# Attention decode on one core: tiles of 8 MB with 64 KB rows in a ring of three, shared by K, V and the projection weights

## The chip, the cores and the metric

The kernel runs on one core of a Trainium2 chip. The metric is the device time of one execution in microseconds (us), lower is better; a median over several executions is quoted. The profile's span is about 2 us shorter than the measured time of the same execution (2602.3 against 2604.1 us for the kernel before).

In the text, PE is the matmul engine, VectorE (DVE in the profile) does elementwise work and reductions, ScalarE (ACT) does exp and copies, SP is the engine whose queue issues the loads. "The DMA" means the 16 DMA engines that move data from HBM, the main memory, into SBUF, the memory on the core (128 partitions, its rows).

## The reference

Two independent problems A and B of the same shape; the outputs are concatenated. Every query attends to 4096 cached keys.

```python
B, Sq, D = 8, 1, 1024
H, Sk, Dh = 32, 4096, 128          # all bf16

def _A_ref(x, k_cache, v_cache, wq, wo):
    q = (x @ wq).reshape(B, Sq, H, Dh).transpose(0, 2, 1, 3)
    scores = jnp.einsum("bhqd,bhkd->bhqk", q, k_cache) * (Dh ** -0.5)
    p = softmax(scores, axis=-1)
    o = jnp.einsum("bhqk,bhkd->bhqd", p, v_cache)
    return o.transpose(0, 2, 1, 3).reshape(B, Sq, H * Dh) @ wo
# B_ref is the same on its own inputs; result: concatenate([a, b], axis=-1)
```

The caches are 4 x 268 MB, and wq and wo are 4 x 8.4 MB. Each byte is used once, so the kernel has to read 1107 MB.

## The kernel before

A tile holds four heads of one batch entry: 128 partitions, 32 partitions a head, T = 128 keys of 128 values in each partition, so 32 KB a partition and 4 MB a tile. K and V tiles alternate through a ring of five slots. One transfer loads one tile, and it may start when the tile that held the slot before, five tiles ago, has been used up:

```python
HQ = 4; MP = 128 // HQ; T = Sk // MP; CT = 32; NR = T // CT    # four chunks a tile
NSLOT = 5
order = [("k", 0)]
for n in range(NQ - 3):
    order += [("k", n + 1), ("v", n)]
...
def freed(i):                       # what has to be done before a slot is loaded anew
    kind, n = order[i]
    return opEacc.get(NR * n + NR - 1) if kind == "k" else opPV.get((n, NR - 1))
...
from_ = caches[c][...][b, hb * HQ:(hb + 1) * HQ].rearrange("u (m t) d -> (u m) (t d)", m=MP)
op = dma(to, from_, ("t", i % NSLOT), [dep])                   # 128 rows of 32 KB
```

For each of the chunks of a K tile, VectorE multiplies by q in place, reduces the partial sums of the chunk before, and folds 128 products to 64; PE sums the 64 to 16 with four identity matmuls. K's slot is free when the last chunk's matmuls have read it:

```python
make_mul(s)            # VectorE: ring *= q           128x4096
make_red(s - 1)        # VectorE: 16 partial sums to 1, of the chunk before
fold = make_fold(s)    # VectorE: ring[:64] += ring[64:]
...
make_eacc(s, fold)     # PE: red += identity @ ring, four times; the last reader of the chunk
```

The softmax follows on ScalarE, then PE multiplies by V. The weights have buffers of their own and come in rows of 2 KB: wq in 8 pieces of 2 MB, wo in 16 pieces of 1 MB.

```python
opWQ[m] = dma(WQ[:], caches[c][3][:, col:col + HM * Dh].rearrange("(k p) n -> p k n", p=128), ...)
opWO[blk] = dma(WO[:], caches[c][4][hb * HQ * Dh:(hb + 1) * HQ * Dh, :].rearrange("(h p) n -> p h n", p=128), ...)
```

Of the kernel before, what the change touches and what calls it, by code (L numbers as in the profile page):

```python
# [81 lines left out]

def _build_kernel(nc, caches, out):
# [3 lines left out]
    assert B == 8 and Sq == 1 and Dh == 128 and Sk == 4096 and D == 1024 and H % 8 == 0  # L87
    DC = D // 128
    scale = float(Dh) ** -0.5
    HQ = 4  # L90
# [4 lines left out]
    HM = 2 * HQ  # L95
    MPC = H // HM
    NM = NC * MPC
    NB = NC * H // HQ
    NQ = NB * B
    NS = NQ * NR  # L100
    NSLOT = 5
    PL = 7
    RG = T // 4 // 4

    es = ExitStack()
    with es:
# [3 lines left out]

        ident = sb("ident", [128, 128], BF16)
        mask = sb("mask", [128, HQ], FP32)
        E16 = sb("E16", [128, 4, HQ], BF16)
        selb = sb("selb", [B, B, MP], BF16)
        x_sb = sb("x_sb", [B, NC, D], BF16)
        xT = sb("xT", [128, NC * DC * B], BF16)
        WQ = sb("WQ", [128, DC, HM * Dh], BF16)
        WO = sb("WO", [128, HQ, D], BF16)
        q_sb = sb("q_sb", [B, 4, HQ * Dh], BF16)
        qbc = sb("qbc", [128, 2, Dh], BF16)  # L120
        ring = sb("ring", [128, NSLOT, T * Dh], BF16)
        s_sb = sb("s_sb", [128, 3, T], FP32)
        rmax = sb("rmax", [128, 2], FP32)
        ngm = sb("ngm", [128, 2], FP32)
        bias = sb("bias", [128, 2], FP32)
        rsum = sb("rsum", [128, 2, B], FP32)
        PM = sb("PM", [128, 3, T, HQ], BF16)
        accS = sb("accS", [128, 2, 512], BF16)
        rl = sb("rl", [128, 2, HQ * B], FP32)
        on_sb = sb("on_sb", [128, 2, HQ, B], BF16)  # L130
        orow = sb("orow", [64, 512], BF16)

        red_ps = [ps(f"red{i}") for i in range(2)]
        pv_ps = [ps(f"pv{i}") for i in range(2)]
        o_ps = [ps(f"o{i}") for i in range(2)]
        misc = ps("misc")
        proj = ps("proj")
        misc_bf16 = misc.bitcast(BF16)

        sems = {e: es.enter_context(nc.semaphore(f"c_{e}")) for e in ENGINES[1:]}  # L140
        for name, n in (("t", NSLOT), ("vl", NR), ("wq", 1), ("wo", 1), ("x", 1), ("out", 1)):
            for i in range(n):
                sems[(name, i)] = es.enter_context(nc.semaphore(f"{name}{i}"))
# [4 lines left out]
        def dma(out_ap, in_ap, key, deps):  # L148
            return add("sp", lambda e: e.dma_start(out_ap, in_ap), deps, dma_key=key)


        def pool_select(view, base, pattern, dep):
            return add("pool", lambda e: e.affine_select(out=view, in_=view, compare_op=ALU.not_equal, fill=1.0,
                                                         base=base, pattern=pattern, channel_multiplier=1), [dep])
        z = [add("pool", lambda e, m=m: e.memset(m[:], 0.0)) for m in (ident, selb, E16, mask)]
        c_ident = pool_select(ident[:], 0, [[-1, 128]], z[0])
        c_selb = pool_select(selb[:], 0, [[-1, B], [0, MP]], z[1])

        c_E16 = z[2]
        for q in range(4):  # L160
            c_E16 = pool_select(E16[:], -32 * q, [[-4, 4], [-1, HQ]], c_E16)
        c_mask = z[3]
        for j in range(HQ):
            c_mask = add("dve", lambda e, j=j: e.memset(mask[MP * j:MP * (j + 1), j:j + 1], 1.0), [c_mask])
        c_PM = add("pool", lambda e: e.memset(PM[:], 0.0))
        c_pv = [add("dve", lambda e, t=t: e.memset(t[:], 0.0)) for t in pv_ps]

        opT, opMul, opEacc, opRed, opRmax, opNgm, opBias, opExp = {}, {}, {}, {}, {}, {}, {}, {}
        opPV, opAcc, opExt, opQb, opQbc, opQ, opQs, opWQ, opWO = {}, {}, {}, {}, {}, {}, {}, {}, {}
        opLsum, opNorm, opProj = {}, {}, {}  # L170
        last = {"misc": None}
        outs = []



        order = [("k", 0)]
        for n in range(NQ - 3):
            order += [("k", n + 1), ("v", n)]
        order += [("k", NQ - 2), ("k", NQ - 1), ("v", NQ - 3), ("v", NQ - 2), ("v", NQ - 1)]
# [6 lines left out]
        def freed(i):  # L186

            kind, n = order[i]
            return opEacc.get(NR * n + NR - 1) if kind == "k" else opPV.get((n, NR - 1))

        def load_tiles():
            while issued[0] < len(order):
                i = issued[0]
                dep = None
                if i >= NSLOT:
                    dep = freed(i - NSLOT)
                    if dep is None:
                        return
                kind, n = order[i]
                blk, b = divmod(n, B)  # L200
                c, hb = divmod(blk, H // HQ)
                from_ = caches[c][1 if kind == "k" else 2][b, hb * HQ:(hb + 1) * HQ].rearrange("u (m t) d -> (u m) (t d)", m=MP)
                to = tile_of(kind, n)
                if i == len(order) - 1:
                    for r in range(NR):
                        cols = slice(r * CT * Dh, (r + 1) * CT * Dh)
                        opT[("v", n, r)] = dma(to[:, cols], from_[:, cols], ("vl", r), [dep])
                else:
                    op = dma(to, from_, ("t", i % NSLOT), [dep])
                    for r in range(NR):  # L210
                        opT[(kind, n, r)] = op
                issued[0] += 1

        def load_wq(m):
            c, p = divmod(m, MPC)
            col = p * HM * Dh
            opWQ[m] = dma(WQ[:], caches[c][3][:, col:col + HM * Dh].rearrange("(k p) n -> p k n", p=128),
                          ("wq", 0), [_at(opQ, (m - 1, 1))])

        def load_wo(blk):  # L220
            c, hb = divmod(blk, H // HQ)
            opWO[blk] = dma(WO[:], caches[c][4][hb * HQ * Dh:(hb + 1) * HQ * Dh, :].rearrange("(h p) n -> p h n", p=128),
                            ("wo", 0), [_at(opProj, blk - 1)])


        def make_q(m, f):

            c = m // MPC
            blk = 2 * m + f

            def emit(e):
                for k in range(DC):
                    i = e.matmul(misc[0:B, :], xT[:, (c * DC + k) * B:(c * DC + k + 1) * B],  # L233
                                 WQ[:, k, f * HQ * Dh:(f + 1) * HQ * Dh], start=(k == 0), stop=(k == DC - 1))
                return i
            opQ[(m, f)] = add("pe", emit, [c_xT, opWQ[m], last["misc"]])
            opQs[blk] = last["misc"] = add(
                "act", lambda e: e.activation(q_sb[:, blk % 4, :], misc[0:B, :], ACTF.Copy),  # L238
                [opQ[(m, f)], _at(opQb, (blk - 4) * B + B - 1)])

        def make_qbc(n):

            blk, b = divmod(n, B)

            def emit(e):
                for j in range(HQ):
                    i = e.matmul(misc[MP * j:MP * (j + 1), 0:Dh], selb[:, b, :], q_sb[:, blk % 4, j * Dh:(j + 1) * Dh],  # L247
                                 start=True, stop=True, tile_position=(0, MP * j))
                return i
            opQb[n] = add("pe", emit, [c_selb, opQs[blk], last["misc"]])  # L250
# [18 lines left out]
        def make_eacc(s, fold):  # L269
            v = chunk(*divmod(s, NR)).rearrange("p (t j w) -> p t j w", j=8, w=16)  # L270
# [6 lines left out]
            opEacc[s] = add("pe", emit, [fold, c_ident, _at(opRed, s - 2)])  # L277

        def make_red(s):
            n, r = divmod(s, NR)  # L280
            opRed[s] = add("dve", lambda e: e.tensor_reduce(  # L281
                s_sb[:, n % 3, r * CT:(r + 1) * CT], red_ps[s % 2][:, :].rearrange("p (t w) -> p t w", w=16), AX.X, ALU.add),
                [opEacc[s]] + _at(opExp, n - 3, []))


        def make_rmax(n):
            opRmax[n] = add("dve", lambda e: e.tensor_reduce(rmax[:, n % 2:n % 2 + 1], s_sb[:, n % 3, :], AX.X, ALU.max),  # L287
                            [opRed[NR * n + NR - 1]])

        def make_ngm(n):  # L290
            opNgm[n] = add("dve", lambda e: e.tensor_reduce(  # L291
                ngm[:, n % 2:n % 2 + 1], rmax[:, n % 2:n % 2 + 1].to_broadcast([128, 32]), AX.X, ALU.max,
                negate=True, apply_transpose=True), [opRmax[n], _at(opBias, n - 2)])

        def make_exp(n):
            blk, b = divmod(n, B)
            opBias[n] = add("act", lambda e: e.activation(bias[:, n % 2:n % 2 + 1], ngm[:, n % 2:n % 2 + 1], ACTF.Copy, scale=scale),  # L297
                            [opNgm[n]] + _at(opExp, n - 2, []))
            opExp[n] = []
            for j in range(HQ):  # L300
                rows = slice(MP * j, MP * (j + 1))

                def emit(e, j=j, rows=rows):
                    return e.activation(PM[rows, n % 3, :, j], s_sb[rows, n % 3, :], ACTF.Exp, bias=bias[rows, n % 2:n % 2 + 1],  # L304
# [187 lines left out]
```

## Time and profile before

| | before |
|---|---|
| time, median | 2603.8 us (2603.3 to 2604.4) |
| HBM read | 1107 MB, 426 GB/s over the span |
| VectorE / PE / ScalarE busy | 80% / 53% / 17% |
| packets of the DMA | 54,248 |

From the page of the kernel before. The first two lines are the busy tenths of VectorE and of the DMA in 40 slices of the span, then what the DMA moved in each slice, its packets, and the chain of waits by engine. Of the groups (line, engine, operation, tiles, count, busy us, mean ns, idle us before it and what ended it) two are shown, and of the issues (queue, count, size, median us from issue to landing) the loads of K and V.

```profile
DVE  7778887788878878788787887878878788788887
DMA  9999999999999999999999999999999999999997
GB/s 410 427 429 430 431 427 429 431 429 432 425 430 431 430 429 428 431 429 432 429 424 431 430 430 431 427 430 432 429 431 421 428 433 427 433 429 431 430 430 314
DMA packets 54248, 1108.58 MB, mean 426 GB/s; under 512 B 4577, under 2 KB 4609, under 8 KB 21009
...
DMA 70%; DVE 22%; PE 7%; ACT 1%; issue 1%; SPq 0%
...
L262 DVE TENSOR_TENSOR ring<-ring,qbc 128x4096 bf16<-128x4096 bf16 x512 | 1165.9, 2277 | 476.0 <-DMA ring<-in_A_k_cache_dram 247.4
...
L304 ACT ACTIVATE PM<-s_sb,bias 32x128 bf16<-32x128 f32 x512 | 295.0, 576 | 15.1
...
ring<-in_A_k_cache_dram SPq DMA_DIRECT2D x64, 4096.0 KB, 39.9
ring<-in_A_v_cache_dram SPq DMA_DIRECT2D x64, 4096.0 KB, 31.4
```

The DMA is busy in every slice, and VectorE's idle time, 476 us, ends on landings of K: the DMA is the limit. A K tile takes 9.7 us to move, but it lands 39.9 us after its issue. So it is issued while about three other tiles still stand in the queue before it. The queue is never near dry.

The trace also holds each packet of the DMA with its bytes and duration. A row of a tile is one packet:

```
bytes of a packet   count    mean ns
 2,048              16,400      88
32,768              32,640    1219
```

### The profile page before, as it was taken

How to read it: one execution, taken by the hardware profiler on the slowest of the kernel's cores; microseconds unless marked ns; L12 is line 12 of the kernel's file. 1: busy time of each engine (PE TensorE's matmuls, PEld its weight loads, DVE VectorE, ACT ScalarE, POOL GpSimd, SP SyncE). 2: the span in 40 equal slices, each digit the busy share in tenths (PEclk: the TensorE clock that was granted, in tenths of full speed). 3: DMA queues.
4: the chain of work that ended last, by engine and by line, in shares of the span. 5: the costliest groups of instructions: out<-in, count | busy, mean ns of one | idle time of the engine just before them, and what ended most of it. 6: DMA issues, size and time to landing. Idle time of an engine off the chain costs nothing.

```text
span 2602.3 us, 18878 instructions
## 1 busy us (share of the span) xinstructions
PE 1383.7 (53%) x7568; PEld 384.3 (15%) x7568; DVE 2086.1 (80%) x1833; ACT 445.7 (17%) x1427; POOL 3.6 (0%) x15
## 2 busy tenths in 40 slices
PE   4455564554545555455554555545555455454555
PEld 1111111111111111111111111111111111111111
DVE  7778887788878878788787887878878788788887
ACT  1112111121111111121111211112111121121112
POOL 0000000000000000000000000000000000000000
PEclk8666666666666667666666666666666666666666
DMA  9999999999999999999999999999999999999997
GB/s 410 427 429 430 431 427 429 431 429 432 425 430 431 430 429 428 431 429 432 429 424 431 430 430 431 427 430 432 429 431 421 428 433 427 433 429 431 430 430 314
DMA packets 54248, 1108.58 MB, mean 426 GB/s; under 512 B 4577, under 2 KB 4609, under 8 KB 21009
## 3 DMA queue, kind: packets, MB, share of 16 engines
q1 hardware_dynamic: 54160, 1107.38, 99.5%
q8 instruction: 59, 0.97, 0.2%
q14 instruction: 29, 0.23, 0.0%
HBM read 1107.33 MB, written 0.03 MB: 426 GB/s over the span
## 4 chain that ended last, share of the span: by engine, by line
DMA 70%; DVE 22%; PE 7%; ACT 1%; issue 1%; SPq 0%
DMA ring<-in_B_k_cache_dram 31%; DMA ring<-in_A_k_cache_dram 30%; DVE ring L262 12%; DVE ring L267 6%; DMA ring<-in_A_v_cache_dram 4%; DMA ring<-in_B_v_cache_dram 4%; PE red L275 3%; DVE s_sb L281 3%; PE pv L317 2%; ACT PM L304 1%; PE proj L357 1%; PE o L338 0%; PE misc L233 0%; DVE rmax L287 0%; ACT accS L323 0%
## 5 line engine op out<-in xcount | busy, mean ns | idle before, releaser
L262 DVE TENSOR_TENSOR ring<-ring,qbc 128x4096 bf16<-128x4096 bf16 x512 | 1165.9, 2277 | 476.0 <-DMA ring<-in_A_k_cache_dram 247.4
L275 PE MATMUL red<-ring,ident 128*128 128x512 bf16 x2048 | 887.2, 583 | 992.2 <-DVE ring L267 992.2
L267 DVE TENSOR_TENSOR ring<-ring 128x2048 bf16<-128x2048 bf16 x512 | 622.0, 1215 | 0.0
L275 PEld LDWEIGHTS red<-ring,ident 128*128 128x128 bf16 x2048 | 214.3, 127 | 1461.9 <-DVE ring L267 1204.1
L317 PE MATMUL pv<-ring,PM 128*16 128x512 bf16 x4096 | 398.7, 505 | 7.1 <-DMA ring<-in_A_v_cache_dram 4.5
L281 DVE TENSOR_REDUCE s_sb<-red 128x32 f32<-128x512 f32 x512 | 350.0, 684 | 16.7 <-PE red L275 16.7
L297 ACT ACTIVATE bias<-ngm 128x1 f32<-128x1 f32 x128 | 26.0, 203 | 1590.2 <-DVE ngm L291 1590.2
L304 ACT ACTIVATE PM<-s_sb,bias 32x128 bf16<-32x128 f32 x512 | 295.0, 576 | 15.1
L331 PE MATMUL o<-E,accS 128*128 128x4 bf16 x512 | 34.1, 171 | 206.0 <-ACT accS L323 205.9
L317 PEld LDWEIGHTS pv<-ring,PM 128*16 128x16 bf16 x4096 | 99.6, 101 | 282.1 <-issue 236.8
L304 ACT ACTIVATION_READ_ACCUMULATOR PM<-s_sb,bias 32x1 f32 x512 | 128.1, 250 | 0.0
L252 ACT ACTIVATE qbc<-misc 128x128 bf16<-128x128 f32 x128 | 35.5, 278 | 385.9 <-PE misc L247 385.9
L323 ACT ACTIVATE accS<-pv 128x512 bf16<-128x512 f32 x128 | 76.4, 597 | 6.2 <-PE pv L317 2.8
L331 PEld LDWEIGHTS o<-E,accS 128*128 128x128 bf16 x512 | 23.5, 107 | 314.2 <-ACT accS L323 314.2
L287 DVE TENSOR_REDUCE rmax<-s_sb 128x1 f32<-128x128 f32 x128 | 36.6, 286 | 4.5
L247 PE MATMUL misc<-q_sb,selb 8*32 8x128 bf16 x512 | 37.3, 282 | 0.8 <-ACT q_sb L238 0.8
L233 PE MATMUL misc<-WQ,xT 128*8 128x512 bf16 x128 | 32.8, 402 | 6.2 <-DMA WQ<-in_A_wq_dram 6.2
L238 ACT ACTIVATE q_sb<-misc 8x512 bf16<-8x512 f32 x16 | 9.4, 587 | 143.1 <-PE misc L233 143.1
L247 PEld LDWEIGHTS misc<-q_sb,selb 8*32 8x32 bf16 x512 | 13.4, 96 | 106.5 <-issue 106.5
L338 PE MATMUL o<-rsum,mask 128*128 128x8 f32 x128 | 28.9, 354 | 0.0
L338 PEld LDWEIGHTS o<-rsum,mask 128*128 128x128 f32 x128 | 27.7, 319 | 0.0
L291 DVE TRANSPOSE_TENSOR_REDUCE ngm<-rmax 128x1 f32<-128x32 f32 x128 | 26.2, 204 | 0.0
(25 smaller groups left out, 59.2 us busy)
## 6 DMA issues: line engine op xcount, KB each, us to landing
ring<-in_A_k_cache_dram SPq DMA_DIRECT2D x64, 4096.0 KB, 39.9
ring<-in_A_v_cache_dram SPq DMA_DIRECT2D x64, 4096.0 KB, 31.4
ring<-in_B_k_cache_dram SPq DMA_DIRECT2D x64, 4096.0 KB, 40.4
ring<-in_B_v_cache_dram SPq DMA_DIRECT2D x63, 4096.0 KB, 31.8
WQ<-in_A_wq_dram SPq DMA_DIRECT2D x4, 2048.0 KB, 41.5
WO<-in_A_wo_dram SPq DMA_DIRECT2D x8, 1024.0 KB, 38.1
WQ<-in_B_wq_dram SPq DMA_DIRECT2D x4, 2048.0 KB, 44.3
WO<-in_B_wo_dram SPq DMA_DIRECT2D x8, 1024.0 KB, 37.6
```

The source lines that it names most:

```text
L247: i = e.matmul(misc[MP * j:MP * (j + 1), 0:Dh], selb[:, b, :], q_sb[:, blk % 4, j * Dh:(j + 1) * Dh], start=True, stop=True, tile_position ...
L252: "act", lambda e: e.activation(qbc[:, n % 2, :], misc[:, 0:Dh], ACTF.Copy),
L262: opMul[s] = add("dve", lambda e: e.tensor_tensor(v, v, qbc[:, n % 2, :].unsqueeze(1).to_broadcast([128, CT, Dh]), ALU.mult), [opT[("k", n ...
L267: return add("dve", lambda e: e.tensor_tensor(v[:, :, 0:64], v[:, :, 0:64], v[:, :, 64:128], ALU.add), [opMul[s]])
L275: i = e.matmul(dst, ident[:], v[:, :, j, :], start=(j == 0), stop=(j == 3))
L281: opRed[s] = add("dve", lambda e: e.tensor_reduce(s_sb[:, n % 3, r * CT:(r + 1) * CT], red_ps[s % 2][:, :].rearrange("p (t w) -> p t w", w ...
L287: opRmax[n] = add("dve", lambda e: e.tensor_reduce(rmax[:, n % 2:n % 2 + 1], s_sb[:, n % 3, :], AX.X, ALU.max), [opRed[NR * n + NR - 1]])
L304: return e.activation(PM[rows, n % 3, :, j], s_sb[rows, n % 3, :], ACTF.Exp, bias=bias[rows, n % 2:n % 2 + 1], scale=scale, accum_out=rsum ...
L317: i = e.matmul(bank[32 * q:32 * q + 4 * HQ, :], PM[:, n % 3, t:t + 4, :].rearrange("p t j -> p (t j)"), v[:, t * Dh:(t + 4) * Dh], start=( ...
L323: opAcc[n] = add("act", lambda e: e.activation(accS[:, n % 2, :], pv_ps[n % 2][:], ACTF.Copy), [opPV[(n, NR - 1)], _at(opExt, n - 2)])
L331: x = e.matmul(o_ps[blk % 2][:, HQ * b:HQ * (b + 1)], accS[:, n % 2, i * 128:(i + 1) * 128], E16[:, i, :], start=(i == 0), stop=(i == 3))
L338: x = e.matmul(o_ps[blk % 2][:, 64 + B * j:64 + B * (j + 1)], mask[:, j:j + 1].to_broadcast([128, 128]), rsum[:, blk % 2, :], start=True, ...
```

## The change

The intent is longer rows. A tile becomes eight heads of one batch entry, 16 partitions a head: 64 KB a partition and 8 MB a tile, in eight chunks of the same size as before. Only three such slots fit in SBUF, and wq and wo have no room of their own any more. They go through the ring too, each whole weight matrix as one tile with rows of 64 KB. The last eight heads of the last wo stay apart (2 MB in rows of 2 KB), so the second wo is loaded into 96 partitions only. Around this the softmax changes form: exp runs eight times over 128 partitions, with a scale of 0 and a bias of -200 for partitions of other heads, instead of four times over 32.

```diff
-    HQ = 4
+    HQ = 8
...
-    NSLOT = 5
-    PL = 7
+    NSLOT = 3
...
-        order = [("k", 0)]
-        for n in range(NQ - 3):
-            order += [("k", n + 1), ("v", n)]
-        order += [("k", NQ - 2), ("k", NQ - 1), ("v", NQ - 3), ("v", NQ - 2), ("v", NQ - 1)]
+        order = [("wq", 0), ("k", 0)]
+        late = {}
+        for n in range(NQ):
+            if n == 0:
+                order += [("wq", c) for c in range(1, NC)]
+            if n + 1 < NQ:
+                order.append(("k", n + 1))
+            for c in range(NC):
+                if n == done_at(c, NC, HB, B) + 1:
+                    order.append(("wo", c))
+                    late[n] = c
+            if n == NQ - 1:
+                order.append(("wo8", 0))
+            order.append(("v", n))
...
+                elif kind == "wq":
+                    opT[(kind, n)] = dma(to[:, 0:DC * H * Dh], caches[n][3].rearrange("(p k) n -> p (k n)", k=DC), key, [dep])
+                elif kind == "wo":
+                    rows = wo_rows(n)                     # 128 for the first, 96 for the second
+                    opT[(kind, n)] = dma(to[0:rows, 0:H * D], caches[n][4][0:rows * H, :].rearrange("(p r) n -> p (r n)", r=H),
+                                         key, [dep])
...
+                    cuts = [0, NR]
+                    if n == NQ - 1:                       # only the last K and V are cut into pieces
+                        cuts = [0, NR // 2, NR] if kind == "k" else [0, NR // 2, 3 * NR // 4, 7 * NR // 8, NR]
...
+            opRmax[n] = add("dve", ... tensor_reduce(rmax[:], s_sb[:, n % 2, :], AX.X, ALU.max), ...)
+            t = add("dve", ... tensor_scalar(rtmp..., half..., rmax[:, 0:1], None, ALU.add), ...)
+            opNgm[n] = add("dve", ... tensor_reduce(ngm[:], rtmp[:], AX.X, ALU.max, negate=True, apply_transpose=True), [t])
+            opBias[n] = add("dve", ... scalar_tensor_tensor(bias[:, n % 2, :], own_sc[:], ngm[:, 0:1], own_b[:], ...), ...)
...
-        pv_at = {max(NR * v + PL, NS + 2 * (v - NQ + 3) if v >= NQ - 3 else 0): v for v in range(NQ)}
+        pv_at = {((n + 2, 0) if n in late else (n + 1, 5)): n for n in range(NQ - 1)}
```

(Cuts marked by "..."; the shapes of the masks, of exp, of the projections and of the output are left out.)

## The prediction

> **What bounds it now.** The DMA. The page's slices show the 16 DMA engines nine tenths busy or more until the last slice, at about 430 GB/s; VectorE is busy 80%, PE 53%; the chain of waits is 70% DMA. VectorE's real idle time, 476 us in the groups, ends on landings of K tiles. The Trainium skill ("DMA: Bandwidth & Descriptors", section "Where 436 GB/s comes from") puts the ceiling at 435 GB/s; this trace stays just under it. So 1107 MB cannot take less than 2545 us, and a gain over 2% (under 2552 us) is out of reach.
>
> **What the change is worth in the DMA.** The trace's packet records: a 32 KB packet (one row of a tile) takes 1218 ns, a 2 KB packet (a row of wq or wo) 88 ns. The line through both gives 27.2 GB/s an engine and about 13 ns a packet, 3 ns of it overlapped.
> - 16,400 packets of 2 KB become some 500 of 64 KB, beside 1,024 that stay: 960 packets an engine at 10 ns, about 9 us less.
> - 32,768 rows of 32 KB become 16,384 of 64 KB: 1,024 packets an engine, about 10 us less, if a row stays one packet. If it is cut in two: zero.
> - Half the semaphore packets (4,577 of 9 ns): 1 us.
> Together 10 to 20 us, all on the critical path.
>
> **What it adds.** VectorE does the same products, folds and reductions (3.93 us a chunk). The maximum is taken half as often but by four dependent instructions: I estimate 1.3 us per 8 MB tile against 0.45 per 4 MB now. exp becomes 8 activations of 128x256 per tile (0.7 us each, estimated from 0.58 for 128); ACT stays mostly idle.
>
> **Does a ring of three keep the DMA full?** K is freed 32.8 us of VectorE plus 1.9 us of PE after landing, 34.7 us; issue to first byte is 1.4 us (seen at the last store). The two tiles behind it take 2 x 19.4 = 38.8 us. So 2.7 us of slack: the DMA stays full, but the queue runs nearly dry each cycle (issue to landing falls to about 22 us for V, 42 for K). VectorE waits about 6 us for each K. The engines now drift apart (they finish up to 10 us apart); the ring will hold the early ones back, which costs nothing, as the slowest sets the pace.
>
> **One-off gaps.** Start: the second wq's 64 matmuls delay the freeing of the first K by some 6 us, a DMA gap near 2 us. End: the last V may load only after the last K is freed, while V and wo before it take 24 us: a gap near 6 us. The tail after the last landing shrinks from 10 us to about 7, thanks to smaller last pieces.
>
> **Sum.** 2604 - 20 (DMA) + 8 (gaps) - 4 (tail) = 2588 us; 2598 if rows are cut. Range 2576 to 2612. Faster by over 2%: 1%; within 2%: 94%; slower: 5%.
>
> **What would show it.** Packets near 21,000 instead of 54,248; mid-run 432 to 434 GB/s; slices all nine until the end; a dip in the last slices; VectorE idle before the K product about 400 us, ended by DMA.
>
> **What would make it wrong.** If freeing K takes over 37.5 us, or issuing is slower behind queued transfers, every cycle gains a DMA gap: each microsecond costs 64 us, and 2 us over makes it slower by more than 2%. VectorE stalls behind the PV matmuls, now 32 a chunk, could do that. 64 KB rows could also move at another rate.

## The result, and the profile after

| | before | after |
|---|---|---|
| time, median | 2603.8 us | 2635.1 us (2632.6 to 2642.0) |
| ratio, 95% interval | | 1.0124 (1.0105 to 1.0144) |
| GB/s over the span | 426 | 421 |
| packets of the DMA | 54,248 | 20,840 |

A ratio is the mean time of one kernel's fast runs over that of the other's in the same rounds, so it is not quite the ratio of the medians. The change made the kernel 1.2% slower, and the predicted range (2576 to 2612 us) missed the time by 23 us.

The lines of the page of the kernel after that answer to those above:

```profile
DVE  3788788888888888788885888888887887858885
DMA  9999999999999999999999999999999999999997
GB/s 415 430 430 426 428 420 429 429 429 424 415 433 425 428 429 416 427 430 421 430 428 429 432 418 434 431 425 430 432 429 427 418 428 430 420 330 431 428 421 303
DMA packets 20840, 1108.61 MB, mean 421 GB/s; under 512 B 2272, under 2 KB 2336, under 8 KB 3376
...
DMA 55%; DVE 36%; PE 6%; ACT 1%; issue 1%; SPq 0%; DVEq 0%
...
L299 DVE TENSOR_TENSOR ring<-ring,qbc 128x4096 bf16<-128x4096 bf16 x512 | 1170.1, 2285 | 464.8 <-DMA ring<-in_A_k_cache_dram 234.8
...
L340 ACT ACTIVATE PM<-s_sb,bias,own_sc 128x256 bf16<-128x256 f32 x512 | 609.3, 1607 | 894.6 <-DVE bias L333 894.6
...
ring<-in_A_k_cache_dram SPq DMA_DIRECT2D x32, 43.3
ring<-in_A_v_cache_dram SPq DMA_DIRECT2D x32, 24.2
```

The packets fell as predicted (near 21,000). VectorE's idle time before the product, predicted at about 400 us, is 464.8. Three things more did not follow.

First, the rate in the middle is 415 to 434 GB/s where a steady 432 to 434 was expected, and VectorE's share of the chain of waits rose from 22% to 36%. The last line says why this may be: a V tile takes 19.4 us to move and lands 24.2 us after its issue. About 5 us is all the warning that the queue gets. The "9" of every slice hides it, for a packet that starts slowly counts as busy.

Second, one slice stands at 330 GB/s.

Third, the dip at the end is there, but larger than predicted.

How one cycle goes, from the timeline (start, duration, engine, line, operation, [idle before and what ended it]). VectorE, kernel after:

```profile
515.80 2.29 DVE L299 TENSOR_TENSOR ring<-ring,qbc 128x4096 bf16<-128x4096 bf16 x1 [5.44 <-DMA ring<-in_A_k_cache_dram]
...
547.40 1.21 DVE L304 TENSOR_TENSOR ring<-ring 128x2048 bf16<-128x2048 bf16 x1
555.29 2.29 DVE L299 TENSOR_TENSOR ring<-ring,qbc 128x4096 bf16<-128x4096 bf16 x1 [6.68 <-DMA ring<-in_A_k_cache_dram]
```

PE, the same stretch, the matmuls of the last chunk:

```profile
548.67 1.89 PE L313 MATMUL red<-ring,ident 128*128 128x512 bf16 x4 [2.40 <-DVE ring L304]
```

The issuing queue, the same stretch:

```profile
550.59 0.33 SPq L162 DMA_DIRECT2D ring<-in_A_v_cache_dram  x1
550.96 0.43 SPq L162 DMA_DIRECT2D ring<-in_A_k_cache_dram  x1
```

K lands at 515.8, VectorE ends its last fold at 548.6, PE's matmuls end at 550.56, and at once the next V is issued. That is 34.8 us after the landing, as the prediction had it (34.7). But the next K starts at 555.29, 39.5 us after this one, where two tiles at full rate would take 38.7.

The packet records show what lies between. (Their clock was laid over the engines' by setting the last semaphore write of a K load to the start of VectorE's first product on it.) In the kernel after the median 64 KB packet takes 2418 ns, that is 12 ns less than two median packets of 32 KB (1215 ns), but the mean is 2461: of the 829 packets between 100 and 2290 us that took over 100 ns longer than that, 600 started 1 to 5 us after the issue of a V. They are the first packets of that V, with a median of 2880 ns. An instance with the queue just dry: the first wo, which has the same rows, was issued at 1341.32 with the V behind it, its packets on the waiting engines start about 1.4 us later and take 2.9 to 3.4 us; the packets that start where those end take 2418 to 2420 ns again. So a late issue costs twice, in engines that stand idle and in first packets that take longer: 0.46 us in the median of the 600, 0.5 to 1 us in this instance.

Sorted by how long before the first DMA engine ran dry the V was issued ("lead"), the 61 V loads took, on the mean of the 16 engines:

```
lead of the issue    V loads    us from the tile before it to this V
under 1 us             10        20.58
1 to 2 us              22        20.09
2 to 3 us              20        19.58
3 us and more           9        19.38
```

A tile at full rate takes 19.35 us. With a lead of 3 us nothing is lost; the mean lead was 2.0 us (1.9 if the start and the end of the run are left out, as in the table of doses below).

### The profile page after: what moved, and what is told of

Read it like the earlier page. It is cut to its first block, busy times and chain, and to the rows that moved or that the text cites. A ratio compares the mean times of both kernels' runs of the same rounds, so it can differ in the third digit from the quotient of the medians.

```text
span 2633.7 us, 19575 instructions
## 1 busy us (share of the span) xinstructions
PE 1256.2 (48%) x8130; PEld 380.7 (14%) x8130; DVE 2100.2 (80%) x1807; ACT 675.4 (26%) x1169; POOL 5.7 (0%) x23
## 2 busy tenths in 40 slices
DMA packets 20840, 1108.61 MB, mean 421 GB/s; under 512 B 2272, under 2 KB 2336, under 8 KB 3376
## 4 chain that ended last, share of the span: by engine, by line
DMA 55%; DVE 36%; PE 6%; ACT 1%; issue 1%; SPq 0%; DVEq 0%
DMA ring<-in_A_k_cache_dram 26%; DMA ring<-in_B_k_cache_dram 25%; DVE ring L299 19%; DVE ring L304 10%; DVE s_sb L321 5%; PE red L313 4%; PE pv L352 2%; DMA ring<-in_B_v_cache_dram 2%; DMA ring<-in_B_wo_dram 1%; ACT PM L340 1%; DMA ring<-in_A_wq_dram 1%; PE q L263 1%; DVE rmax L327 1%; SPq L162 0%; DVE rtmp L329 0%
## 5 line engine op out<-in xcount | busy, mean ns | idle before, releaser
L299 DVE TENSOR_TENSOR ring<-ring,qbc 128x4096 bf16<-128x4096 bf16 x512 | 1170.1, 2285 | 464.8 <-DMA ring<-in_A_k_cache_dram 234.8
L313 PE MATMUL red<-ring,ident 128*128 128x512 bf16 x2048 | 845.8, 559 | 1293.7 <-DVE ring L304 1290.9
L340 ACT ACTIVATE PM<-s_sb,bias,own_sc 128x256 bf16<-128x256 f32 x512 | 609.3, 1607 | 894.6 <-DVE bias L333 894.6
L304 DVE TENSOR_TENSOR ring<-ring 128x2048 bf16<-128x2048 bf16 x512 | 622.0, 1215 | 0.0
L321 DVE TENSOR_REDUCE s_sb<-red 128x32 f32<-128x512 f32 x512 | 349.9, 683 | 30.8 <-PE red L313 30.6
L352 PE MATMUL pv<-ring,PM 128*32 128x512 bf16 x4096 | 326.4, 475 | 21.1 <-DMA ring<-in_B_v_cache_dram 21.1
L360 ACT ACTIVATE accS<-pv 128x512 bf16<-128x512 f32 x64 | 38.2, 597 | 885.9 <-PE pv L352 885.9
L340 ACT ACTIVATION_READ_ACCUMULATOR PM<-s_sb,bias,own_sc 128x1 f32 x512 | 255.6, 499 | 0.0
L352 PEld LDWEIGHTS pv<-ring,PM 128*32 128x32 bf16 x4096 | 115.0, 115 | 239.0 <-issue 186.0
L263 PE MATMUL q<-ring,xT 128*8 128x512 bf16 x128 | 25.9, 411 | 19.6 <-DMA ring<-in_A_wq_dram 19.6
L373 PE MATMUL o<-accS,E 128*32 128x32 bf16 x896 | 31.7, 177 | 0.0
L373 PEld LDWEIGHTS o<-accS,E 128*32 128x32 bf16 x896 | 25.9, 94 | 24.2 <-ACT accS L360 14.0
L327 DVE TENSOR_REDUCE rmax<-s_sb 128x1 f32<-128x256 f32 x64 | 26.9, 420 | 2.2
L333 DVE SCALAR_TENSOR_TENSOR bias<-own_sc,ngm,own_b 128x8 f32<-128x8 f32 x64 | 14.5, 226 | 2.3
## 6 DMA issues: line engine op xcount, KB each, us to landing
ring<-in_A_v_cache_dram SPq DMA_DIRECT2D x32, 24.2
```

Of the source, the lines that this page charges most:

```text
L263: i = e.matmul(q_ps[f][rows, :], xT[:, (c * DC + k) * B:(c * DC + k + 1) * B], w[:, col:col + 512], start=(k == 0), stop=(k == DC - 1), ti ...
L299: opMul[s] = add("dve", lambda e: e.tensor_tensor(v, v, qbc[:, n % 2, :].unsqueeze(1).to_broadcast([128, CT, Dh]), ALU.mult), [opT[("k", n ...
L304: return add("dve", lambda e: e.tensor_tensor(v[:, :, 0:64], v[:, :, 0:64], v[:, :, 64:128], ALU.add), [opMul[s]])
L313: i = e.matmul(dst, ident[:], v[:, :, j, :], start=(j == 0), stop=(j == 3))
L321: opRed[s] = add("dve", lambda e: e.tensor_reduce(s_sb[:, n % 2, r * CT:(r + 1) * CT], red_ps[s % 2][:, :].rearrange("p (t w) -> p t w", w ...
L327: opRmax[n] = add("dve", lambda e: e.tensor_reduce(rmax[:], s_sb[:, n % 2, :], AX.X, ALU.max), [opRed[NR * n + NR - 1]])
```

## The experiments

**Theory A** (late issue): the loss is that V is issued too short a time before the queue runs dry, because K's slot is freed 34.8 us after landing and only two tiles stand behind it. **Theory B**: these transfers start slowly whenever they are issued. **Theory C**: rows of 64 KB are slow in themselves. **Theory D** concerns the slice at 330 GB/s: a load into 96 partitions is slow by its shape.

In the expectations, "the changed kernel" is the kernel after.

### Half of each V issued 16 us earlier

```diff
+                    two = order[i][0] == "v" and order[i][1] < NQ - 1 and prev[0] == "k"
+                    if two and i not in first:
+                        dep = opEacc.get(NR * prev[1] + NR // 2 - 1)   # chunks 0 to 3 of the K in this slot
...
+                        first[i] = dma(tile_of("v", n)[:, 0:NR // 2 * CT * Dh], from_[:, 0:NR // 2 * CT * Dh], ("t", i % NSLOT), [dep])
...
-                    cuts = [0, NR]
+                    cuts = [NR // 2, NR] if i in first else [0, NR]
```

> The changed kernel, but each V (except the last) is loaded as two halves of its columns, and the first half is issued as soon as the first four chunks of the K in its slot are done, about 16 us earlier. Theory A (late issue: V is issued on average 1.9 us before the fastest DMA engine runs dry, and a transfer needs about 3 us of lead): the queue no longer runs dry, landings come every 19.4 to 19.5 us instead of 19.7, about 29 us less: 2606 us, 2598 to 2614. Theory B (every transfer of this kind starts slowly, whenever it is issued): more transfers, so no gain: 2635 us or more. Theory C (64 KB rows are slow): half of the loss goes with half of the rows: about 2620 us.

Measured: 2612.4 us (2612.1 to 2613.1), 22.7 us less than the kernel after, as theory A has it. From its page:

```profile
GB/s 418 431 434 432 428 433 434 428 433 436 428 432 432 431 433 435 430 428 438 429 413 427 438 432 427 434 433 427 433 434 428 433 437 428 408 336 431 428 433 303
```

The middle now stands at 427 to 438 GB/s but for two slices (413 with the first wo, 408 before the second); the slice of the second wo (336) and the end are as before. (Single slices overshoot, since the page books a packet whole in the slice in which it starts; over 131 us the packet records give 432.) A half of V lands 9.71 us after the load before it, and K 19.35 us after that. The median time from one K to the next fell from 39.18 to 38.78 us. And the 16 DMA engines now finish a load up to 8 us apart, 4.7 in the median, instead of 2.6 in the kernel after, and nothing is lost by it. Theories B and C would have had nothing, or half, of this.

### The same halves, issued late

```diff
+                    if kind == "v" and n < NQ - 1:
+                        dma(to[:, 0:NR // 2 * CT * Dh], from_[:, 0:NR // 2 * CT * Dh], key, [dep])
+                        cuts = [NR // 2, NR]
```

> Control for the run before: the same two halves of each V, but both are issued only when the whole slot is free, as in the changed kernel. Theory A: no gain; 8 more packets an engine and V cost about 5 us in all: 2635 to 2645 us. Theory B: slower, up to 2660. Theory C (64 KB rows are slow): about 2620 us.

Measured: 2638.7 us (2635.7 to 2646.5). The halves alone bring nothing; the gain of the run before came from the early issue. Theory C, which had 2620 us here, falls.

### K freed earlier: less work on VectorE

```diff
-            fold = make_fold(s)
+            fold = opMul[s] if r in (1, 3) else make_fold(s)
```

> Wrong result on purpose: the folding product is left out in two of the eight chunks of every K, so that VectorE is done 2.3 us earlier and the slot is freed 2.3 us earlier; the loads are unchanged. Theory A: mean lead 1.9 becomes about 4.2 us, beyond the 3 us needed: about 25 to 29 us less, 2606 us (2600 to 2616). Theories B and C: the DMA sets the time and is unchanged, 2630 to 2640 us.

Measured: 2609.3 us (2607.5 to 2610.8), 25.8 us less, with the very transfers of the kernel after. (Part of each score is left out; the output still passed the comparison with the reference.) From its page:

```profile
GB/s 419 433 433 433 433 431 427 429 433 432 428 434 428 431 432 433 434 432 433 431 429 433 431 431 432 431 432 433 430 432 432 433 434 432 427 328 434 433 429 301
```

Between the first slice and the second wo this is 427 to 434 GB/s, close to the 432 to 434 that the prediction expected, from a change that touches no transfer. Theory B falls with it.

### K freed later: more work on VectorE

```diff
+            if r == 3 and n >= 1:
+                x = opBias[n - 1]
+                for _ in range(3):
+                    x = add("dve", lambda e, n=n: e.tensor_reduce(rmax[:], s_sb[:, (n - 1) % 2, :], AX.X, ALU.max), [x])
```

> Dose in the other direction: three needless reductions on VectorE in each K (1.2 us), so that the slot is freed 1.2 us later; VectorE still has some 6 us of idle time per K, so it doesn't become the limit by its sum. Theory A: lead falls to 0.7 us, 0.6 to 1.2 us lost in each of 63 cycles: 2635 + 38 to 76 = 2673 to 2711 us. Theories B and C: unchanged, 2630 to 2640 us.

Measured: 2661.6 us (2658.3 to 2664.8). The direction is theory A's, and B and C are out, but the size is below the expected range: 26.5 us instead of 38 to 76. The three doses side by side, between 100 and 2290 us of each trace:

```
                     K's first product     lead of V over     first packets over
                     to V's issue, mean    the first engine   100 ns slow       time
less on VectorE       32.69 us              3.13 us            149             2609.3 us
after                 34.92 us              1.88 us            600             2635.1 us
more on VectorE       36.10 us              1.42 us            597             2661.6 us
```

The lead fell by 0.46 us where the freeing came 1.2 us later. A cycle that loses time also moves the end of the queue back (39.36 to 39.66 us from one K to the next, on the mean), and the 16 engines finished the tile before closer together (2.65 to 2.23 us from the first to the last), so the lead shrinks less than the freeing is delayed. The expectation had left this out.

### The kernel before with three slots, and with four

```diff
-    NSLOT = 5
+    NSLOT = 3
```

> The kernel before (4 MB tiles, rows of 32 KB), with a ring of 3 slots instead of 5, nothing else. Theory A: a K is freed some 18.3 us after it lands and the two tiles behind it take 19.4 us, so loads are issued about as the queue runs dry: 1.3 us or more lost in each of 127 cycles of 19.4 us: 2604 + 165 or more = 2770 us (2720 to 2830). A theory in which the row of 64 KB or the tile of 8 MB is at fault leaves this kernel near 2604 us (at most 2620).

Measured: 2721.2 us (2719.0 to 2730.0), ratio 1.0459 (1.0440 to 1.0479). The kernel before, with its 32 KB rows and 4 MB tiles, loses 117 us by the depth of the ring alone; the size is at the lower end of the expected range. From its page:

```profile
GB/s 404 414 406 413 417 414 412 409 409 410 409 416 416 419 407 417 403 417 403 409 370 417 411 412 403 419 411 409 416 408 417 417 409 395 418 412 413 408 416 303
```

The loads of this kernel, from its page (count, size, median us from issue to landing):

```profile
ring<-in_A_k_cache_dram SPq DMA_DIRECT2D x64, 4096.0 KB, 22.3
ring<-in_A_v_cache_dram SPq DMA_DIRECT2D x64, 4096.0 KB, 13.5
```

With `NSLOT = 4`:

> The kernel before with a ring of 4 slots instead of 5. Theory A: three tiles of 9.7 us lie behind a K that is freed after 18.3 us, so a load is issued more than 9 us before the queue runs dry, and nothing is lost: 2604 us, within 6 us. If each slot taken away costs by itself (3 slots cost 117 us), some 50 us more: 2650 us.

Measured: 2603.1 us (2603.0 to 2603.3), ratio 1.000 (0.998 to 1.002). Its loads:

```profile
ring<-in_A_k_cache_dram SPq DMA_DIRECT2D x64, 4096.0 KB, 21.5
ring<-in_A_v_cache_dram SPq DMA_DIRECT2D x64, 4096.0 KB, 30.1
```

The fifth slot was idle insurance, and the fourth is worth 118 us. A tile takes 9.7 us to move, so with three slots a V is issued 3.8 us before its own transfer can begin, and with four slots the shortest such time, that of K, is 11.8 us. It isn't slots or bytes that count but whether the load is issued before the queue is dry.

### What long rows are worth

```diff
-                    op = dma(to, from_, ("t", i % NSLOT), [dep])
+                    mid = NR // 2 * CT * Dh
+                    dma(to[:, 0:mid], from_[:, 0:mid], ("t", i % NSLOT), [dep])
+                    op = dma(to[:, mid:], from_[:, mid:], ("t", i % NSLOT), [dep])
```

> The kernel before (ring of 5, queue always full), but every K and V is loaded as two halves of its columns issued together: rows of 16 KB instead of 32 KB, 2,040 more packets for each DMA engine. It measures the gain that the prediction ascribed to long rows, in the other direction: at 10 ns a packet, 20 us more: 2624 us (2620 to 2630). If a packet costs nothing: 2604 us.

Measured: 2622.6 us (2622.2 to 2623.0), 19.3 us more for 2,040 more data packets an engine, 9.5 ns a packet (with 255 more semaphore packets of 9 ns in it). The gain that the prediction ascribed to long rows, 10 ns a packet, is real and was sized right.

### The second wo with 128 partitions

The slice at 330 GB/s is that load. PE's wait for it, and the issues, in the kernel after:

```profile
2337.50 2.30 PE L420 MATMUL proj<-ring,on_sb 96*8 96x256 bf16 x40 [5.63 <-DMA ring<-in_B_wo_dram]
```

```profile
2304.44 0.33 SPq L162 DMA_DIRECT2D ring<-in_B_wo_dram  x1
2304.81 0.43 SPq L162 DMA_DIRECT2D ring<-in_B_v_cache_dram  x1
2348.54 0.33 SPq L162 DMA_DIRECT2D ring<-in_B_k_cache_dram  x1
```

It was issued at 2304.4; by the packet records the tile before it landed at 2307.3 and it landed itself at 2336.9: 29.6 us for 6.3 MB, where 6 packets an engine at 2.42 us make 14.5 us. (The semaphore events put both 0.3 to 0.6 us later, 29.9 us apart.) Its packets took mostly 4.7 to 5.1 us, twice the usual.

```diff
-                    opT[(kind, n)] = dma(to[0:rows, 0:H * D], caches[n][4][0:rows * H, :].rearrange("(p r) n -> p (r n)", r=H),
+                    opT[(kind, n)] = dma(to[:, 0:H * D], caches[n][4].rearrange("(p r) n -> p (r n)", r=H),
```

> The changed kernel, but the second wo is loaded with all 128 partitions (8 MB) instead of 96 (6 MB); the 32 extra rows aren't used. Theory D (a load into 96 partitions runs at half rate: it took 29.6 us for 6.3 MB, packets of some 5 us instead of 2.4[...]): the larger load lands 19.4 us after the tile before it, so the time falls by about 10 us: 2625 us (2620 to 2630). Theory E (that load was late because it was issued 0.3 us after the fastest engine had run dry, and it is slow for no reason of its shape): the larger load takes longer, not shorter: 2635 to 2640 us.

Measured: 2625.4 us (2623.7 to 2626.2), 9.7 us less although 2 MB more are moved. From its page, the slice that stood at 330:

```profile
GB/s 417 430 430 429 419 430 422 431 432 429 421 430 430 426 422 417 430 431 430 422 430 419 432 431 433 418 431 427 432 422 428 427 424 430 431 420 429 418 430 293
```

In the packet records the load now takes 21.1 us instead of 29.6. So the loss was of the shape (theory D), and not of the late issue (theory E), which would have made the larger load take longer. The Trainium skill ("SBUF — State Buffer", section "Door 1: The DMA port swizzle") says that the rate depends on how many of 16 ports into SBUF a transfer's partitions reach. By that section's table partitions 0 to 95 reach all 16, so the count alone doesn't foretell the half rate that was measured here. Why 96 partitions were slow stays open: no run here shows the ports.

### The PV matmuls moved out of K's way

```diff
-        pv_at = {((n + 2, 0) if n in late else (n + 1, 5)): n for n in range(NQ - 1)}
+        gap = set(range(NQ - 2))
+        pv_at = {((n + 2, 0) if n in gap else (n + 1, 5)): n for n in range(NQ - 1)}
...
-                if k == 1 and v in late:
+                if k == 1 and v in gap:
```

> The changed kernel, but the probabilities times V are multiplied in one burst of 64 matmuls between two K tiles, where VectorE and PE wait for the next K, instead of in two bursts of 32 behind chunks 4 and 5 of a K. Theory A (issue too late): the bursts hold up VectorE for 30.6 us in all (its waits for the reduction matmuls), about 0.5 us per cycle; without them K is freed 0.5 us earlier, and by the slope of the dose runs (0.4 us per cycle for 1.2 us) about 10 us come back: 2625 us (2618 to 2632). Were it PE's bursts alone that made the loss: about 2606 us. Theory B: unchanged, 2635 us.

Measured: 2639.7 us (2637.4 to 2643.8), no gain: a miss. The reason lies before the time: V's issue did not move, with a median of 34.78 us after K's first product against 34.82 in the kernel after. The waits of VectorE for PE (us in all, times, the longest), in the kernel after and in this run:

```profile
DVE s_sb L321 <- PE red L313: 30.6, 34, 5.6
DVE s_sb L321 <- PE red L313: 23.9, 13, 6.6
```

The expectation had spread 30.6 us evenly over the cycles, but most of it lies in a few long waits that stayed. In the cycles that hold no weights VectorE ended its last fold 0.23 us earlier (32.97 us after K's first product instead of 33.20, means of 54 and 56 cycles). From there to V's issue it then took 0.21 us longer (1.96 instead of 1.75 us): the last four matmuls of a K took 1.04 us in a quarter of the cycles of the kernel after, and here in one of 54. Why they are sometimes faster, no run shows. So the run doesn't speak against theory A (what it was to make earlier stayed where it was), and it settles a smaller thing: the bursts of 32 matmuls, which the prediction named as a danger, held VectorE up by about 0.2 us a K, and moving them brought nothing.

### A version with all of it

V in early halves, the last V in its four pieces as early as the chunks of the last K allow, and the second wo with 128 partitions.

```diff
+                    if order[i] == ("v", NQ - 1):
...
+                        while len(lastv) < 4:
+                            g = len(lastv)
+                            dep = opEacc.get(NR * prev[1] + cuts[g + 1] - 1)
+                            if dep is None:
+                                return
...
+                            lastv.append(dma(tile_of("v", NQ - 1)[:, cols], from_[:, cols], ("vl", g), [dep]))
```

> Candidate: halves of V issued early as in the first run, the last V in its four pieces as early as the chunks of the last K allow, and the second wo loaded with 128 partitions. Theories A and D: 2612 from the first run, less 10 for wo and 5 for the gap before the last V (the gap is 9 us, but exp of the last tile then sets the end): 2597 us (2592 to 2602), 0.3% faster than before.

Measured: 2597.3 us (2596.9 to 2598.8), ratio to the kernel before 0.9976 (0.9961 to 0.9991): 37.7 us less than the kernel after, and faster than both, though by 0.24% only against the kernel before. From its page:

```profile
GB/s 420 428 436 432 427 436 433 427 436 434 425 435 432 430 437 432 427 434 435 428 407 434 435 428 432 436 427 433 436 427 432 438 425 431 435 407 434 432 431 337
```

The gains add up: 22.7 (early halves) + 9.7 (wo) leave 5.3 us for the end. Its last data landed at 2583.5 us, but exp of the last tile ended only at 2582.5, so none of the 64 PV matmuls could start before; they took 6.3 us from 2583.2. ScalarE and these matmuls now set the end, and not the DMA.

## Why the prediction was wrong

1. **The DMA is the limit and a gain over 2% is all but excluded: right.** The best version stands at 2597 us. At the full rate of these traces (a tile of 8.39 MB in 19.35 us) 1107 MB would take 2554 us, an estimate, and 2% less than before is 2552.
2. **Gain of long rows, 10 ns a packet: right.** 9.5 ns a packet in the test with half rows; 64 KB rows stay one packet (2418 ns, against 2 x 1215).
3. **"So 2.7 us of slack: the DMA stays full": this is the step that failed.** Its two terms differ in how they held. "Freed 34.7 us after landing" was right (34.9 on the mean). "Issue to first byte is 1.4 us" was right as a number (the same was seen with the queue dry) and wrong as the cost of a late issue. First packets after such an issue take longer (0.46 us in the median of the slow ones), and here the load had to be issued some 3 us before the first engine ran dry; it was issued 1.9 to 2.0 us before, on the mean. The slack was also counted from the slowest of 16 engines, and the first was done some 2.6 us before the last (leads of 1.9 and 4.5 us). So the alarm that the prediction had set itself, a freeing in over 37.5 us, stood too high: the loss was there at 34.9 us, and all but gone at 32.7.
4. **"The ring will hold the early ones back, which costs nothing, as the slowest sets the pace": wrong, or at least not free.** K came every 39.4 us on the mean (39.2 in the median) instead of 38.7. Freeing K 2.2 us earlier gave 25.8 us back, issuing V early 22.7 us, although its halves pay for 8 more packets an engine in each V. How it comes about is argued and not shown, as the packet records don't name the engine: a slow first packet sets an engine back in one cycle, it may strike another in the next, and in this ring all wait for the slowest of each cycle, while in a deep queue an engine that fell back can catch up.
5. **The second wo was not in the sum.** The prediction counted its packets and missed its shape: 29.6 us instead of 14.5, 15 us, of which 9.7 came back with 128 partitions. (The 2 MB more that this moves take about 4.8 us at full rate, an estimate from 19.35 us a tile.)
6. **One-off gaps: right in kind, small in size.** Before the last V the DMA stood for 9.3 us on the mean of its engines (predicted 6), since the last V was issued at 2604.44 when the tile before it had landed at 2597.6. At the start there was no gap (the first V landed 19.4 us after the tile before it; predicted 2), and the tail took 7.4 us (predicted 7).
7. **exp at 0.7 us each: wrong, without effect but at the very end.** An activation of 128x256 has a mean of 1.61 us and follows the one before after 1.14 us. ScalarE is busy 26% of the span.

The predicted 2588 us and the missing terms: 27 us for late issues (the 22.7 of the first experiment and some 4.5 us that its extra packets cost, an estimate from 8 x 59 packets of 9.5 ns, as 59 of the V loads came in early halves), 15 us for the second wo and some 2.5 us at the ends (a gap of 9.3 us and a tail 2.8 us shorter, where 8 and 4 were predicted) make some 2633 us, against 2635 measured. The sum was made after the fact.

Not settled: why a first packet takes longer, and why a load into 96 partitions is slow.

## What to carry to other kernels

In a kernel bound by the DMA, ask of every slot how long before the queue runs dry its next load is issued, and read it from the profile as the median time from issue to landing less the time that the load itself takes: 5 us was too little in the kernel after, and 4 us in the one before with three slots; 12 us was enough with four slots. What lies between, no run here shows. Larger tiles in fewer slots free memory in larger steps, and this can cost more than longer rows bring; freeing a slot in parts, as its chunks are used, gives the lead back for a few more packets. And give loads all 128 partitions, even where some rows aren't used: here, in one load, this gave 9.7 us.

## What the Trainium skill lacked or had wrong

- "DMA: Bandwidth & Descriptors", section "Rules for kernel authors", says to issue early, not how early: here a lead of under 1 us cost 1.2 us a load, 2 to 3 us cost 0.2 us, and 3 us none.
- The same page, section "Latency and other measured facts", gives about 600 ns to the first byte for loads issued from SP. Here, by the packet records, the first packet starts about 1.4 us after the start of the issue, and first packets of 64 KB then take 2.9 to 3.4 us instead of 2.42.
- No page has a time measured for cutting a long row into more packets. Here halving the rows of 32 KB cost 9.5 ns for each further packet of an engine. ("DMA: Bandwidth & Descriptors", section "Bandwidth", has about 10.5 ns a packet for loads issued from GpSimd, but that is the time of one 4 KB transfer divided by all its 64 packets, not by those of one engine.)
- "SBUF — State Buffer", section "Door 1: The DMA port swizzle", has rates for up to 64 partitions and for 128, but none for 96. 96 partitions with 64 KB each took 29.6 us (213 GB/s), more than 128 partitions with 64 KB each (21.1 us in the same place), although by its table the 96 reach as many ports.
- "ScalarE: Activation LUTs", section "What ACT_TABLE_LOAD costs", gives an activation 280 ns + 0.833 ns an element and 93 ns for a second pointer operand, so an estimate of some 590 ns for 256 elements. Here exp with bias, scale and sum of 128x256 took 1607 ns, with 1.14 us from one to the next. No run here took it apart.
